# Two feed-forward networks after window attention: every network operation placed by a list scheduler at build time, one accumulator seeded by ScalarE, six weight pieces under attention

## The chip, the cores and the metric

The kernel runs on one core of one Trainium2 chip. The metric is the device time of one execution in microseconds (us); shorter is better. TensorE (PE in the profile; PEld is its weight load), VectorE (DVE), ScalarE (ACT), GpSimd (POOL) and the DMA queue of SyncE (SP) each work through their own instructions strictly in the order in which the program issued them. Semaphores tie the engines together: an instruction whose input isn't there stops everything behind it on its engine.

## The reference

Attention (4 batches, 8 heads, 512 local and 32 global tokens of dimension 64), then two feed-forward networks on its 2176 x 512 result.

```python
def _attn_ref(q_l, k_l, v_l, q_g, k_g, v_g):
    # window 32, scale 1/8; sm is a softmax over the last axis
    out_g = np.matmul(sm(scale * np.matmul(q_g, k_all.transpose(0, 1, 3, 2))), v_all)
    s_ll = np.where(mask, scale * np.matmul(q_l, k_l.transpose(0, 1, 3, 2)), -1000000000.0)
    s_l = np.concatenate([scale * np.matmul(q_l, k_g.transpose(0, 1, 3, 2)), s_ll], axis=-1)
    out_l = np.matmul(sm(s_l), np.concatenate([v_g, v_l], axis=2))
    return np.concatenate([out_g, out_l], axis=2).astype(np.float32)

def _moe_ref(x, w_in, w_out):        # network 1: 512 -> 2048 -> 512
    h = x @ w_in
    return (h * np.cos(h) @ w_out).astype(np.float32)

def _moe2_ref(x, w_in, w_out):       # network 2: the same sizes
    h = np.maximum(x @ w_in, 0.0)
    return (h * h @ w_out).astype(np.float32)
```

The weights arrive as 64-bit floats. Each 64-bit number is put together to a 32-bit one on the chip.

## The kernel before

**Attention.** A loop of 40 items (`s` in the code; 32 local halves and 8 global ones) issues, per turn and in the order of `CFG["order"]`, the stages of several items that are a few turns apart. In between it issues background work from three tables, `bga`, `bgb` and `bgc`: twelve of the 64 *pieces* of weights, the splitting of the first weights, and the preparation of the first block of x.

**A piece** (`conv_load`, `conv_a`, `conv_b`, `conv_c`) is 128 x 512 weights: a DMA of 512 KB into one of two `raw` tiles; POOL scales the high words into `cu` (line 123) and ACT the low words into `cc` (126); DVE shifts `cu` (132) and joins the sign to `cc` (133); POOL adds both into `wf` (142). Four pieces make a pair of chunks `q` (two of `w_in`, two of `w_out`), and there are 16 pairs, eight for each network.

**Splitting.** Every product runs in three passes over a high and a low part of its operands. `prep_in` makes four sums of weight blocks (`ws`, line 171), then high parts on ACT (184) and low parts by subtraction in the helper `split` (150) on DVE or POOL; `prep_out` does the same for `w_out` (`wo`). For x, `x_sum`, `x_hi`, `x_lo` do it (`xr`, `xs`), and the seven split tiles are stored to DRAM (`x_store`) and loaded again (`x_load`) for every later round over the same block. Each of the seven tiles has one buffer.

**Steps.** 48 steps follow: 8 rounds `K` (four for each network) x 3 blocks of x (2 x 384, 2 x 384 and 2 x 320 tokens) x 2 pairs `q`. A step has seven products of six matmuls (line 765), a scheme with fewer products and more additions, into four PSUM banks a, e, b, d. Between them stand additions on DVE (`add`, 779) and copies on ACT (`copy`, 773): after product 2 DVE adds `1` into b, ACT copies b to `2`, and product 4 may go on in b only after that. Each of the four results passes through `unit` (network 1: 795, 798, 803, 809; network 2: 806, 809), then a high part on ACT (818) and a low part on POOL. Then come eight (network 2: six or five) *jobs* of six matmuls (line 858), and DVE adds their results into `xt` (870).

**Order.** `lay` and `run_job` walk once over PE's work with assumed durations and give every operation of a step a time; x preparation, pieces and splitting get times by fixed offsets (`conv_a` 7.0 us after its load, `prep_in` at 2.4 us apart). All are sorted by time and issued so. Two jobs (`BACK = 2`) are held back to fill the next step's gaps. Which engine makes a sum or a low part is fixed.

Of the kernel before, what the change touches and what calls it, by code (L numbers as in the profile page):

```python
# [18 lines left out]
P = 128  # L19
# [31 lines left out]
def kernel(  # L51
# [28 lines left out]
    convp = ctx.enter_context(tc.tile_pool(name="convp", bufs=2))  # L80
# [15 lines left out]

    NQ = 2 * NC // 2
    raw, tmp, wf = {}, {}, {}  # L100
# [3 lines left out]
    def conv_load(q, m, c):  # L104
        g = 2 * q + c
        win, wout = nets[g // NC]
        f0 = (g % NC) * P
        t = convp.tile([P, DM, 2], I32, tag="raw", name="raw", bufs=2)
        flat = t.rearrange("p f w -> p (f w)")
        if m == 0:  # L110
            nc.sync.dma_start(
                flat.rearrange("p (k x) -> p k x", k=NK),
                win[:, 2 * f0 : 2 * f0 + 2 * P].rearrange("(k p) x -> p k x", p=P),
            )
        else:
            nc.sync.dma_start(flat, wout[f0 : f0 + P, :])
        raw[q, m, c] = t

    def conv_a(q, m, c):
        t = raw[q, m, c]  # L120
        u = convp.tile([P, DM], F32, tag="cu", name="cu", bufs=2)
        v = convp.tile([P, DM], U32, tag="cc", name="cc", bufs=2)
        nc.gpsimd.tensor_scalar(  # L123
            u, t[:, :, 1].bitcast(F32), 2.0**-112, 1.0, op0=ALU.mult, op1=ALU.mult
        )
        nc.scalar.activation(v, t[:, :, 0].bitcast(U32), AF.Copy, scale=2.0**-29)  # L126
        tmp[q, m, c] = (u.bitcast(U32), v)

    def conv_b(q, m, c):
        t = raw.pop((q, m, c))  # L130
        u, v = tmp[q, m, c]
        nc.vector.tensor_scalar(u, u, 3, None, op0=ALU.logical_shift_left)  # L132
        nc.vector.scalar_tensor_tensor(  # L133
            v, t[:, :, 1].bitcast(U32), 0x80000000, v,
            op0=ALU.bitwise_and, op1=ALU.bitwise_or,
        )

    def conv_c(q, m, c):
        u, v = tmp.pop((q, m, c))
        if c == 0:  # L140
            wf[q, m] = ringp.tile([P, 2, DM], F32, tag=f"wf{m}", name=f"wf{m}")
        nc.gpsimd.tensor_tensor(wf[q, m][:, c, :].bitcast(U32), u, v, op=ALU.add)  # L142
# [4 lines left out]
    SLOT = {"A11": 0, "A12": 1, "A22": 2, "S1": 3, "S2": 4, "S3": 5, "S4": 6}  # L147
# [4 lines left out]
    def prep_in(q):  # L152
        st = {}

        def sums():
            pool = pools["wa" if q % 3 < 2 else "wb"]
            WI[q] = pool.tile([P, 2, 7 * HALF], F32R, tag=f"wi{q % 3}", name="wi")
            st["s"] = ringp.tile([P, 4, HALF], F32, tag="ws", name="ws")
            f = wf[q, 0].rearrange("p c (h x) -> p c h x", h=2)
            st["f"] = f  # L160

        def s(i):
            f, t = st["f"], st["s"]
            a, b, op = (
                (f[:, 1, 0], f[:, 1, 1], ALU.add),
                (t[:, 0], f[:, 0, 0], ALU.subtract),
                (f[:, 0, 0], f[:, 1, 0], ALU.subtract),
                (f[:, 0, 1], t[:, 1], ALU.subtract),
            )[i]
            eng = nc.vector if i % 2 == 0 else nc.gpsimd  # L170
            eng.tensor_tensor(t[:, i], a, b, op=op)

        def part(k):
            f = wf[q, 0]
            return (
                (slice(0, 2 * HALF), f[:, 0, :]),
                (slice(2 * HALF, 3 * HALF), f[:, 1, HALF:]),
                (slice(3 * HALF, 5 * HALF), st["s"][:, 0:2].rearrange("p i x -> p (i x)")),
                (slice(5 * HALF, 7 * HALF), st["s"][:, 2:4].rearrange("p i x -> p (i x)")),
            )[k]  # L180

        def hi(k):
            w, x = part(k)
            nc.scalar.activation(WI[q][:, 0, w], x, AF.Copy)

        def lo(k):
            w, x = part(k)
            split(nc.gpsimd if k % 2 else nc.vector, WI[q][:, 1, w], x, WI[q][:, 0, w])

        def first():  # L190
            sums()
            s(0)
            s(2)

        def second():
            s(1)
            s(3)
            hi(0)

        def third():  # L200
            lo(0)
            hi(1)
            hi(2)

        def fourth():
            lo(1)
            lo(2)
            hi(3)

        return [first, second, third, fourth, lambda: lo(3)]  # L210

    def prep_out(q):
        def hi(c):
            if c == 0:
                pool = pools["wa" if q % 3 < 2 else "wb"]
                WO[q] = pool.tile([P, 2, 2, DM], F32R, tag=f"wo{q % 3}", name="wo")
            nc.scalar.activation(WO[q][:, 0, c, :], wf[q, 1][:, c, :], AF.Copy)

        def lo(c):
            split(  # L220
                nc.gpsimd if c else nc.vector,
                WO[q][:, 1, c, :], wf[q, 1][:, c, :], WO[q][:, 0, c, :],
            )

        return [lambda: hi(0), lambda: (lo(0), hi(1)), lambda: lo(1)]

# [442 lines left out]
    def it(k):  # L669
# [5 lines left out]
    BLOCKS = ((0, 384), (768, 384), (1536, 320))  # L675
    NG = NQ // 2
    steps = [
        (K, b, 2 * K + i) for K in range(NG) for b in range(len(BLOCKS)) for i in range(2)
    ]
    NS = len(steps)  # L680
    PROD = (
        ("B11", "A11"), ("T1", "S1"), ("T2", "S2"), ("B21", "A12"),
        ("T3", "S3"), ("B22", "S4"), ("T4", "A22"),
    )
    XPOOL = {"B11": "xa", "B21": "xa", "B22": "xa", "T1": "xb", "T2": "xc", "T3": "xc", "T4": "xc"}
    XB, XR, XS = {}, {}, {}
# [4 lines left out]
    def xraw(u, name):  # L691
        c0, n = BLOCKS[u % 3]
# [3 lines left out]
    def x_sum(u, name, kk):  # L696
        n = BLOCKS[u % 3][1]
        if kk == 0:
            XR[u, name] = pools["xb"].tile([P, 2, 384], F32, tag="xr", name="xr", bufs=3)
        src = lambda m: (XR[u, m] if m[0] == "T" else xraw(u, m))[:, kk, 0:n]  # L700
        a, b = {"T1": ("B12", "B11"), "T2": ("B22", "T1"), "T3": ("B22", "B12"), "T4": ("B21", "T2")}[name]
        eng = nc.vector if kk == 0 else nc.gpsimd
        eng.tensor_tensor(XR[u, name][:, kk, 0:n], src(a), src(b), op=ALU.subtract)

    def x_src(u, name):
        n = BLOCKS[u % 3][1]
# [6 lines left out]
    def x_hi(u, name):  # L713
        n = BLOCKS[u % 3][1]
        nc.scalar.activation(x_tile(u, name)[:, 0, :, 0:n], x_src(u, name), AF.Copy)

    def x_lo(u, name, kk):
        n = BLOCKS[u % 3][1]
        t = XB[u, name]
        split(  # L720
            nc.vector if kk == 0 else nc.gpsimd,
            t[:, 1, kk, 0:n], x_src(u, name)[:, kk], t[:, 0, kk, 0:n],
        )

    def x_store(u, name):
        n = BLOCKS[u % 3][1]
        key = net_of(u // 3), u % 3, name
# [3 lines left out]
    def x_load(u, name):  # L731
        n = BLOCKS[u % 3][1]
        t = x_tile(u, name)
        nc.sync.dma_start(
            t[:, :, :, 0:n].bitcast(F32), XS[net_of(u // 3), u % 3, name]
        )


    ops = []

    def at(t, fn):
        ops.append((t, len(ops), fn))

    GT, YB = {}, {}
    YE = 0

    class Step:
        def __init__(self, s):
# [5 lines left out]
            self.bk, self.sb, self.r = {}, {}, {}  # L754

        def prod(self, i, bank_name, start):
            x, a = PROD[i]
            n = self.n
            if start:
                self.bk[bank_name] = ps.tile([P, 512], F32, tag=LB[bank_name], name="h" + bank_name)  # L760
            out, w, xs = self.bk[bank_name][:, 0:n], WI[self.q], XB[self.u, x]
            for k in range(6):
                kk, (ws, xh) = k // 3, ((0, 0), (1, 0), (0, 1))[k % 3]
                c = SLOT[a] * HALF + kk * P
# [5 lines left out]
        def copy(self, bank_name, name):  # L770
            t = pools["s"].tile([P, 384], F32, tag=f"s{name}", name="s" + name)
            self.sb[name] = t[:, 0 : self.n]
            nc.scalar.activation(self.sb[name], self.bk[bank_name][:, 0 : self.n], AF.Copy)  # L773

        def add(self, bank_name, name, to=None):
            src = self.bk[bank_name][:, 0 : self.n]
            if to:
                self.bk[to] = ps.tile([P, 512], F32, tag=LB[to], name="h" + to)
            nc.vector.tensor_tensor(  # L779
                self.bk[to or bank_name][:, 0 : self.n], src, self.sb[name], op=ALU.add  # L780
            )

        def unit(self, t0, bank_name, f, t):

            n, V, A, G = self.n, DV(self.n), DA(self.n), DG(self.n)
            h = lambda: self.bk[bank_name][:, 0:n]
            key = bank_name

            def new_r():
                self.r[key] = pools["s"].tile([P, 384], F32, tag="cr", name="cr", bufs=4)[:, 0:n]  # L790
                return self.r[key]

            def ck():
# [386 lines left out]
```

## Time and profile before

| | us |
|---|---|
| median of 3 runs (933.03 to 938.74) | 935.76 |
| the profiled execution | 935.3 |
| its span, first to last instruction | 933.4 |
| PE busy | 870.1 (93%) |
| DVE busy | 695.8 (75%) |
| POOL busy | 561.3 (60%) |
| ACT busy | 517.4 (55%) |

The span falls into attention (to about 165 us), network 1 (four rounds, to 546 us) and network 2 (to 928 us). Matmuls overlap one another, so PE busy overstates how near PE is to its peak; the time from one matmul's start to the next is what counts. Mean TensorE clock over the span is 0.983 of the higher level (2.4 GHz).

### The profile page before, as it was taken

Reading aid. Unit: us, or ns where it says so; the run is one execution under the profiler, and the core shown is the slowest. Engines: PE = TensorE matmul, PEld = TensorE weight load, DVE = VectorE, ACT = ScalarE, POOL = GpSimd, SP = SyncE. Lnnn points to the kernel's source line nnn. Section 1 sums busy time; section 2 is a strip of 40 time slices with the busy share of each in tenths; the row PEclk is TensorE's granted clock in tenths of the full one; section 3 lists DMA queues with packets and bytes.
Section 4 is the critical chain, followed back from the end, with each engine's and each line's share of the span. In section 5 each row is a group of like instructions: output and inputs, shape, how many; then the busy total and the mean of one; then the engine's idle time right before and its main releaser. Section 6 shows DMA issues by size and latency. Waiting matters only on the chain.

```text
span 933.4 us, 17201 instructions
## 1 busy us (share of the span) xinstructions
PE 870.1 (93%) x6008; PEld 789.0 (85%) x6008; DVE 695.8 (75%) x1495; ACT 517.4 (55%) x1237; POOL 561.3 (60%) x663
## 2 busy tenths in 40 slices
PE   7798987889899999999999799999999999999997
PEld 4577765789899999999999798879888888888885
DVE  6588998489878787878797899876666666675454
ACT  4677876576675656565656465555443534353331
POOL 5498998388646554555455779875554555453231
PEclk9999999899999999999999989999999999999999
DMA  7987933365467655675567166377637863666552
GB/s 167 202 187 186 200 95 107 155 244 179 159 225 282 209 190 188 266 243 186 184 240 261 62 248 232 100 238 262 231 120 239 282 239 117 215 237 221 171 178 57
DMA packets 134311, 182.01 MB, mean 195 GB/s; under 512 B 61008, under 2 KB 114768, under 8 KB 134224
## 3 DMA queue, kind: packets, MB, share of 16 engines
q1 hardware_dynamic: 132048, 180.38, 59.4%
q8 instruction: 48, 0.79, 0.3%
q10 hardware_dynamic: 2176, 0.52, 0.3%
q14 instruction: 39, 0.32, 0.1%
HBM read 141.03 MB, written 35.65 MB: 189 GB/s over the span
## 4 chain that ended last, share of the span: by engine, by line
PE 61%; DVE 18%; POOL 8%; ACT 4%; issue 4%; DMA 2%; SPq 2%; ACTq 0%; DVEq 0%; POOLq 0%
PE y L858 30%; PE hb L765 11%; PE he L765 8%; PE ha L765 7%; POOL g L150 4%; DVE cc L133 2%; DVE pt L422 2%; POOL xs L150 1%; DVE cu L132 1%; PE s L406 1%; DVE cr L809 1%; POOL wf L142 1%; DVE xs L150 1%; ACT g L818 1%; PE o L490 1%
## 5 line engine op out<-in xcount | busy, mean ns | idle before, releaser
L150 POOL TENSOR_TENSOR g<-cr,g 128x384 fp32r<-128x384 f32 (+1 forms) x192 | 193.3, 1008 | 273.9 <-ACT g L818 250.5
L858 PE MATMUL y<-wo,g 128*128 128x512 f32 x816 | 215.7, 398 | 7.1 <-ACT g L818 4.4
L870 DVE TENSOR_TENSOR xt<-y,xt 128x384 f32<-128x384 f32 (+2 forms) x287 | 168.7, 593 | 69.1 <-PE y L858 68.6
L858 PE MATMUL y<-g,wo 128*128 128x384 f32 (+1 forms) x1152 | 218.3, 327 | 0.9 <-POOL g L150 0.9
L858 PEld LDWEIGHTS y<-g,wo 128*128 128x128 f32 x1152 | 194.6, 189 | 1.2 <-POOL g L150 1.2
L765 PE MATMUL hb<-xs,wi 128*128 128x384 f32 (+1 forms) x864 | 169.6, 331 | 15.8 <-ACT s L773 12.1
L858 PEld LDWEIGHTS y<-wo,g 128*128 128x128 f32 x816 | 150.0, 189 | 37.6 <-POOL g L150 7.7
L765 PEld LDWEIGHTS hb<-xs,wi 128*128 128x128 f32 x864 | 147.6, 190 | 26.4 <-ACT s L773 15.6
L818 ACT ACTIVATE g<-cr 128x384 fp32r<-128x384 f32 (+1 forms) x192 | 96.9, 507 | 84.2 <-DVE cr L809 82.9
L765 PE MATMUL he<-xs,wi 128*128 128x384 f32 (+1 forms) x576 | 112.9, 331 | 4.6 <-DVE cr L809 4.5
L765 PE MATMUL ha<-xs,wi 128*128 128x384 f32 (+1 forms) x576 | 111.6, 329 | 0.0
L765 PEld LDWEIGHTS he<-xs,wi 128*128 128x128 f32 x576 | 99.7, 191 | 9.8 <-DVE cr L809 5.9
L765 PEld LDWEIGHTS ha<-xs,wi 128*128 128x128 f32 x576 | 98.5, 189 | 2.3
L142 POOL TENSOR_TENSOR wf<-cu,cc 128x512 uint32<-128x512 uint32 x64 | 85.0, 1329 | 22.6 <-DVE cc L133 22.6
L803 ACT ACTIVATE cr<-cr,halfpi 128x384 f32<-128x384 f32 (+1 forms) x96 | 57.5, 599 | 38.1 <-DVE cr L798 37.5
L773 ACT ACTIVATE s<-hb 128x384 f32<-128x384 f32 (+1 forms) x48 | 22.7, 474 | 95.2 <-DVE hb L779 95.2
L123 POOL TENSOR_SCALAR cu<-raw 128x512 f32<-128x512 f32 x64 | 44.0, 688 | 26.6 <-DMA raw<-in_moe_w_in_dram 17.3
L133 DVE SCALAR_TENSOR_TENSOR cc<-raw,cc 128x512 uint32<-128x512 uint32 x64 | 58.6, 915 | 0.0
L432 ACT ACTIVATE pt<-pt,st 128x160 f32<-128x160 f32 x128 | 53.1, 420 | 6.6 <-DVE st L422 6.3
L132 DVE TENSOR_SCALAR cu<-cu 128x512 uint32<-128x512 uint32 x64 | 46.4, 724 | 6.8 <-POOL cu L123 6.6
L126 ACT ACTIVATE cc<-raw 128x512 uint32<-128x512 uint32 x64 | 42.6, 665 | 7.7 <-DMA raw<-in_moe_w_in_dram 6.1
L422 DVE CUSTOM_DVE_ANT_0 pt<-s,mask 128x160 f32<-128x160 f32 x128 | 33.7, 318 | 16.8 <-PE s L406 16.7
(125 smaller groups left out, 1337.7 us busy)
## 6 DMA issues: line engine op xcount, KB each, us to landing
xs<-xs_T SPq DMA_DIRECT2D x48, 768.0 KB, 5.8
xs<-xs_B SPq DMA_DIRECT2D x36, 768.0 KB, 5.3
raw<-in_moe_w_in_dram SPq DMA_DIRECT2D x32, 512.0 KB, 6.8
raw<-in_moe_w_out_dram SPq DMA_DIRECT2D x32, 512.0 KB, 5.2
xs<-xs_T SPq DMA_DIRECT2D x24, 640.0 KB, 6.5
xs_T<-xs SPq DMA_DIRECT2D x16, 768.0 KB, 4.1
xs<-xs_B SPq DMA_DIRECT2D x18, 640.0 KB, 5.8
xs_B<-xs SPq DMA_DIRECT2D x12, 768.0 KB, 4.0
```

The lines of the kernel that those rows point to most:

```text
L123: nc.gpsimd.tensor_scalar(u, t[:, :, 1].bitcast(F32), 2.0**-112, 1.0, op0=ALU.mult, op1=ALU.mult)
L132: nc.vector.tensor_scalar(u, u, 3, None, op0=ALU.logical_shift_left)
L133: nc.vector.scalar_tensor_tensor(v, t[:, :, 1].bitcast(U32), 0x80000000, v, op0=ALU.bitwise_and, op1=ALU.bitwise_or,)
L142: nc.gpsimd.tensor_tensor(wf[q, m][:, c, :].bitcast(U32), u, v, op=ALU.add)
L150: eng.tensor_tensor(lo, x, hi.bitcast(F32), op=ALU.subtract)
L422: nc.vector.tensor_tensor_reduce(out=self.pt[:, u, :], in0=self.s[u // 2][:, 160 * (u % 2) : 160 * (u % 2) + 160], in1=m, scale=-0.125, sc ...
L432: nc.scalar.activation(self.pt[:, u, :], self.pt[:, u, :], AF.Exp, bias=self.st[:, 0, u : u + 1], scale=-1.0, accum_out=self.st[:, 1, u : ...
L765: nc.tensor.matmul(out, lhsT=w[:, ws, c : c + P], rhs=xs[:, xh, kk, 0:n], start=start and k == 0, stop=k == 5, skip_group_check=True,)
L803: nc.scalar.activation(self.r[key], self.r[key], AF.Sin, bias=halfpi, scale=TWOPI)
L818: nc.scalar.activation(GT[k][0][:, t * n : t * n + n], self.r[key], AF.Copy)
L858: nc.tensor.matmul(o, lhsT=l, rhs=r, start=k == 0, stop=k == 5)
L870: nc.vector.tensor_tensor(dst, y, dst, op=ALU.add)
```

## The change

All operations of the networks, on every engine and on the DMA queue, become `Op` objects with needs, durations and a latest time (counted back from a walk over PE's work). A list scheduler places them in simulated time: an engine that is free takes, of the operations that are ready, the one with the earliest latest time. Sums and low parts may go to DVE or POOL (`opVG`), whichever the plan picks. All are issued in the order of their planned starts. On PE the products keep their order, and jobs stay three behind the rate at which they come in (`KEEP`).

From step 2 on, bank b starts from a copy of bank a that ACT writes straight into it (`seed`), and product 2 accumulates on that; the DVE addition after it and the copy `1` are gone. b and d swap banks from step to step. The weight tile of a pair is cut into four tiles. `conv_a` and `conv_b` become four operations; `cu` is gone, since POOL scales straight into the tile of `wf`. `w_out`'s two pieces have a tile each.

Attention carries six pieces in place of twelve: pair 0 whole and `w_in` of pair 1, loaded every third item. The other six, and the splitting of pair 1's `w_out`, go into the plan. Of the sums of these two pairs one each moves from DVE to POOL. The stores of the first x block are issued at the end of attention, ahead of the plan.

```diff
-    t = convp.tile([P, DM, 2], I32, tag="raw", name="raw", bufs=2)
+    ATT = [(0, 0, 0), (0, 0, 1), (0, 1, 0), (0, 1, 1), (1, 0, 0), (1, 0, 1)]
...
-    def conv_a(q, m, c):
-        u = convp.tile([P, DM], F32, tag="cu", name="cu", bufs=2)
+    def conv_u(q, m, c):
+        u = conv_to(q, m, c)
+        G.tensor_scalar(u, t[:, :, 1].bitcast(F32), 2.0**-112, 1.0, op0=ALU.mult, op1=ALU.mult)
...
+    SEM = 0.2
+    d_mm = lambda n: n * 0.000414 + 0.0147
+    d_act = lambda n: 0.17 + n * 0.00084
+    d_ps = lambda n: 0.14 + n * 0.0011
+    d_v2 = lambda n: 0.2 + n * 0.0018
+    d_g2 = lambda n: 0.1 + n * 0.0024
...
+    def opVG(n, fn, *needs):
+        return Op({"G": d_g2(n), "V": d_v2(n)}, lambda e: fn(V if e == "V" else G), *needs)
+    def opQ(kb, fn, *needs):
+        return Op({"Q": kb / 330.0}, lambda e: fn(), *needs, lag=2.0)
...
+        def seed(self):
+            A.activation(self.hold("b"), self.hold("a"), AF.Copy)
...
+                if i == 0:
+                    if s < SEEDED:
+                        o["s1"] = opA(da, lambda: self.copy("a", "1"), p, free_s.get("1"))
+                    else:
+                        o["s1"] = opA(da, self.seed, p, bank_free.get(B_))
+                elif i == 2:
+                    b = p
+                    if s < SEEDED:
+                        p.after(bank_free.get(B_))
+                        b = free_s["1"] = opV(d1, lambda: self.add("b", "1", "b"), p, o["s1"])
+                    else:
+                        p.after(o["s1"])
+                    o["s2"] = opA(da, lambda: self.copy("b", "2"), b, free_s.get("2"))
+                    o["e"] = opV(d1, lambda: self.add("e", "2", "e"), o["s2"], o["s5"])
+                elif i == 4:
+                    p.after(o["s2"])
+                    o["d"] = opV(d1, lambda: self.add("b", "5", "d"), p, o["s5"], bank_free.get(D_))
...
+    def conv(q, m, c):
+        ld = opQ(525.0, lambda: conv_load(q, m, c), *free)
+        u = opG(0.75, lambda: conv_u(q, m, c), ld, *wfree)
+        s = opA(0.67, lambda: conv_s(q, m, c), ld, *cfree)
+        v = opV(0.76, lambda: conv_v(q, m, c), u)
+        o = opV(1.0, lambda: conv_o(q, m, c), s, u)
+        end = opG(1.33, lambda: conv_c(q, m, c), v, o)
...
+    KEEP = 3
+    def target(s, i):
+        lo, hi = (njobs[s - 1] if s else 0), njobs[s]
+        return lo + (hi - lo) * i / 7.0 - KEEP
...
+        f = free_at[e]
+        t = max(f, min(o.at for o in ready[e]))
+        can = [o for o in ready[e] if o.at <= t]
+        o = min(can, key=lambda o: (o.latest, o.key))
...
+    placed.sort(key=lambda o: (o.start, o.key))
...
-    for i in range(12):
-        q, (m, c) = i // 4, PIECES[i % 4]
-        s = 5 + 2 * i + (i // 4)
+    for i, k in enumerate(ATT):
+        s = 5 + 3 * i
+        put(bga, s, lambda k=k: conv_load(*k))
+        put(bga, s + 2, lambda k=k: conv_u(*k))
+        put(bga, s + 2, lambda k=k: conv_s(*k))
+        put(bgb, s + 3, lambda k=k: conv_v(*k))
+        put(bgb, s + 3, lambda k=k: conv_o(*k))
+        put(bgc, s + 4, lambda k=k: conv_c(*k))
...
+            for m, _, _ in PROD:
+                x_store(0, m)
```

## Rows read from the trace of the kernel before

**Rows 1.** Chain of waits: start us, duration us, what; jobs of 512, 384, 320 columns.

```profile
631.06 1.39 PE y L858 x6
...
291.62 2.08 PE y L858 x12
...
276.60 1.75 PE y L858 x12
```

**Rows 2.** Windows, one round K each: length, busy us (instructions), granted clock, DMA share, GB/s.

```profile
165.30:263.80 98.50, 90.40 (x575) 85.84 (x576) 75.28 (x135) 63.18 (x130) 66.61 (x63) 0.97 0.53 192
263.80:355.20 91.40, 89.69 (x542) 89.11 (x542) 73.95 (x138) 54.53 (x112) 49.67 (x51) 1.00 0.63 223
...
446.60:546.20 99.60, 92.48 (x542) 91.24 (x542) 82.75 (x150) 58.26 (x117) 62.05 (x61) 0.97 0.53 193
546.20:646.20 100.00, 95.21 (x487) 85.06 (x487) 82.11 (x126) 54.96 (x111) 79.33 (x74) 0.97 0.59 203
646.20:738.30 92.10, 90.44 (x458) 79.41 (x457) 62.12 (x102) 40.88 (x87) 49.15 (x51) 1.00 0.63 214
...
830.70:928.40 97.70, 96.20 (x488) 85.09 (x486) 49.30 (x83) 34.00 (x72) 26.33 (x28) 1.00 0.50 160
```

**Rows 3.** Timeline of PE: start, us, instruction [idle time before it, what ended it].

```profile
165.21 0.48 PE L475 MATMUL tg<-ident,pg 128*128 128x128 f32 x1 [4.21 <-ACT tgs L484]
...
348.91 1.14 PE L765 MATMUL hb<-xs,wi 128*128 128x320 f32 x6 [1.68 <-ACT s L773]
...
537.70 1.97 PE L765 MATMUL hb<-xs,wi 128*128 128x320 f32 x6 [5.56 <-ACT s L773]
...
576.79 2.29 PE L765 MATMUL hb<-xs,wi 128*128 128x384 f32 x6 [2.19 <-DVE hd L779]
...
617.70 2.50 PE L858 MATMUL y<-wo,g 128*128 128x512 f32 x4 [2.00 <-ACT g L818]
```

**Rows 4.** Chain of waits from 519 to 541 us, the end of round 3.

```profile
532.35 1.48 DVE cc L133
...
535.70 1.07 DVE xs L150
536.77 0.42 DVE hb L779
```

**Rows 5.** Windows in attention, columns as in rows 2.

```profile
24.60:56.80 32.20, 26.00 (x401) 21.25 (x400) 19.43 (x99) 21.06 (x80) 18.35 (x38) 0.95 0.99 208
56.80:141.20 84.40, 73.75 (x1123) 58.08 (x1122) 79.73 (x288) 67.36 (x240) 79.16 (x134) 0.98 0.68 158
```

**Rows 6.** Groups by form, whole span: count, busy us, mean ns, idle before it.

```profile
L123 POOL TENSOR_SCALAR cu<-raw 128x512 f32<-128x512 f32 x64 | 44.0, 688 | 26.6 <-DMA raw<-in_moe_w_in_dram 17.3 <-DMA raw<-in_moe_w_out_dram 8.1 <-PE ha L765 1.2
...
L142 POOL TENSOR_TENSOR wf<-cu,cc 128x512 uint32<-128x512 uint32 x64 | 85.0, 1329 | 22.6 <-DVE cc L133 22.6
...
L132 DVE TENSOR_SCALAR cu<-cu 128x512 uint32<-128x512 uint32 x64 | 46.4, 724 | 6.8 <-POOL cu L123 6.6
...
L133 DVE SCALAR_TENSOR_TENSOR cc<-raw,cc 128x512 uint32<-128x512 uint32 x64 | 58.6, 915 | 0.0
...
L150 POOL TENSOR_TENSOR wo<-wf,wo 128x512 fp32r<-128x512 f32 x16 | 21.2, 1326 | 0.0
...
L150 DVE TENSOR_TENSOR wo<-wf,wo 128x512 fp32r<-128x512 f32 x16 | 11.9, 743 | 0.0
...
L779 DVE TENSOR_TENSOR hb<-hb,s 128x384 f32<-128x384 f32 x32 | 17.9, 560 | 9.2 <-PE hb L765 8.8 <-issue 0.4
...
L773 ACT ACTIVATE s<-ha 128x384 f32<-128x384 f32 x32 | 15.3, 479 | 5.1 <-PE ha L765 5.1
```

**Rows 7.** Tile raw, 0 to 200 us: DVE's join there, min/median/max ns.

```profile
L133 DVE SCALAR_TENSOR_TENSOR cc<-raw,cc x12: 672/679/876, 39.0 to 134.7; 128x512 uint32<-128x512 uint32 x12
```

**Rows 8.** Tile raw, 265 to 530 us: its DMAs.

```profile
DMA to landing us min/median/max: 3.6/7.6/9.7
```

**Rows 9.** Chain of waits from 20 to 60 us.

```profile
39.96 5.29 DMA raw<-in_moe_w_in_dram
```

More of the change, by code (lines that the diff above doesn't have):

```diff
@@ L149, in split @@
+    SLOT = {a: (i, j) for i, part in enumerate(PARTS) for j, a in enumerate(part)}
     def split(eng, lo, x, hi):
         eng.tensor_tensor(lo, x, hi.bitcast(F32), op=ALU.subtract)
[L152 to L210, printed above, removed]
@@ new lines, in w_in @@
+    def w_in(q):
+        ends = [conv(q, 0, c) for c in range(2)]
+        sums = {}
+        for i, needs in ((0, []), (2, [0]), (1, [0]), (3, [1])):
+            o = opVG(256, lambda eng, i=i: w_sum(q, i, eng), *ends, *[sums[k] for k in needs])
+            if i == 0:
+                o.after(*w_free["ws"])
+            sums[i] = o
+        last = max((s for s in range(NS) if steps[s][2] == q - 3), default=None)
+        used = []
+        for k, i in ((0, 3), (1, 2), (2, 5), (3, 6)):
+            n = HALF * len(PARTS[k])
+            src = ends if k in (0, 3) else [sums[2 * k - 2], sums[2 * k - 1]]
+            h = opA(d_act(n), lambda k=k: w_hi(q, k), *src, prods.get((last, i)))
+            lo = opVG(n, lambda eng, k=k: w_lo(q, k, eng), h)
+            wi_ready[q, k] = lo
+            used.append(lo)
+        w_free["wf0"], w_free["ws"] = used + list(sums.values()), used + list(sums.values())
@@ new lines, in w_out @@
+    def w_out(q):
+        ends = [conv(q, 1, c) for c in range(2)]
+        last = max((s for s in range(NS) if steps[s][2] == q - 3), default=None)
+        lo = []
+        for c in range(2):
+            h = opA(d_act(512), lambda c=c: o_hi(q, c), ends[c], *g_free.get(last, []))
+            if c:
+                h.after(lo[0].needs[0])
+            o = opVG(512, lambda eng, c=c: o_lo(q, c, eng), h)
+            wf1_ring.free[WJ[q, c]] = [o]
+            lo.append(o)
+        wo_ready[q] = Op({"N": 0.0}, lambda e: None, *lo)
@@ new lines @@
+    RJ.update({k: (i % 2, i % 2) for i, k in enumerate(ATT)})
+    WJ.update({(0, 0): 0, (0, 1): 1})
+    XRJ.update({(0, m): j for m, j in (("T1", 0), ("T2", 1), ("T3", 2), ("T4", 0))})
+    xr_ring.i = 1
+    w_out(1)
+    for s in range(NS):
+        K, b, q = steps[s]
+        if s % 2 == 0 and s:
+            x_prep(s // 2)
+        S[s].plan()
+        if K < NG - 1:
+            if s % 6 == 0:
+                w_in(2 * K + 2)
+                w_out(2 * K + 2)
+            elif s % 6 == 5:
+                w_in(2 * K + 3)
+        if K and s % 6 == 0:
+            w_out(2 * K + 1)
@@ new lines @@
+    KEEP = 3
+    njobs = [sum(w.s < s for w in jobs) for s in range(NS + 1)]
+    def target(s, i):
+        lo, hi = (njobs[s - 1] if s else 0), njobs[s]
+        return lo + (hi - lo) * i / 7.0 - KEEP
+    order = [(s, i) for s in range(NS) for i in range(7)]
+    t, j = 0.0, 0
+    for s, i in order:
+        while j < target(s, i):
+            jobs[j].latest = t
+            t += jobs[j].on["P"]
+            j += 1
+        prods[s, i].latest = t
+        t += prods[s, i].on["P"]
+    for w in jobs[j:]:
+        w.latest = t
+        t += w.on["P"]
@@ new lines @@
+    BIAS = 6.0
+    count = len(allops)
+    while count:
+        picks = [(b[0], e, b[1]) for e in ready for b in [best(e)] if b]
+        t, e, o = min(picks, key=lambda x: (x[0], x[2] is None))
+        if o is None:
+            free_at[e] = max(t, free_at[e])
+            continue
+        for x in o.on:
+            if o in ready[x]:
+                ready[x].remove(o)
+        o.start, o.end, o.eng = t, t + o.on[e], e
+        if e != "N":
+            free_at[e] = o.end
+        placed.append(o)
+        count -= 1
+        if e == "P":
+            if nxt < len(order) and o is prods[order[nxt]]:
+                nxt += 1
+            else:
+                jdone += 1
+        for y in o.users:
+            missing[y.key] -= 1
+            if missing[y.key] == 0:
+                release(y)
@@ L1053 @@
     put(bgb, 37, lambda: x_hi(0, "T1"))
-    for kk in range(2):
-        put(bgb, 38, lambda kk=kk: x_lo(0, "T1", kk))
+    for kk, eng in enumerate((V, G)):
+        put(bgb, 38, lambda kk=kk, eng=eng: x_lo(0, "T1", kk, eng))
     L = CFG["lag"]
```

612 lines of the change are left out of this document (360 added, 252 removed).

## The prediction

> **What bounds the kernel now.** I read the windows by round first, then PE's timeline for the gaps, then the chain of waits behind the largest gap, then attention's windows, and last the groups by form for prices.
>
> From one matmul's start to the next a run of six takes 1.39 us at 512 columns, and two runs take 2.08 us at 384 and 1.75 at 320 [rows 1]: 0.232, 0.173 and 0.146 us a matmul. A step of network 1 has 42 + 48 matmuls of one width, 15.6 us at 384 and 13.1 at 320; a step of network 2 has 42 of its width and 36 (30) of 512, 15.6 and 13.1 again. A round has four wide steps and two narrow ones: 88.6 us that nothing in the change touches, 709 us for eight rounds. The rounds fill 165.3 to 928.4 us, 763 us. So 54 us of the networks are gaps or slow matmuls, and that is what an order of instructions can win back.
>
> Where they are [rows 2]: the second round (the third is alike) lasts 91.4 us, 2.8 over the 88.6; the fourth 99.6 (11.0 over), the fifth 100.0 (11.4), the sixth (the seventh is alike) 92.1 (3.5). The first lasts 98.5, but pushes the ten jobs of 320 columns at its end into its successor (60 x 0.146 = 8.8 us), so it is 18.7 over 79.8; the last, 97.7, holds such a rest and is nearly full.
>
> The gaps look alike [rows 3]. Product 4 into b waits 1.68 us (second round) and 5.56 us (fourth) for ACT's copy of b. The chain at the 5.56 us shows who was late: not ACT, but DVE, whose addition into b (0.42 us) stood in its queue behind the join of a piece (1.48 us) and a low part of x (1.07 us) [rows 4], none of them urgent. PE isn't short of work in total, DVE isn't full (74 of 91 us in a round [rows 2]); the order in DVE's queue is wrong for a few us at a time.
>
> In attention it is different: from 56.8 to 141.2 us DVE is busy 79.7 and POOL 79.2 of 84.4 us, PE 73.8 [rows 5]. There the two engines are the bound. Before 56.8 us the DMA queue is: its share is 0.99 [rows 5], and a late load of a piece holds the chain for 5.29 us [rows 9].
>
> **The change, part by part.** The sum is made against the profiled execution's 935.3 us (0.5 below the median; 1.9 us lie outside its span).
>
> *Six pieces leave attention.* A piece costs POOL 0.69 + 1.33 = 2.02 us and DVE 0.72 + 0.92 = 1.64 us [rows 6]. Ten of the twelve lay in the stretch from 56.8 us; four will. Pair 1's `w_out` takes a low part of 1.33 us off POOL and one of 0.74 off DVE [rows 6]; two sums of half that width go from DVE to POOL, by half those prices 0.4 and 0.7 us each. POOL: 79.2 - 12.1 - 1.3 + 1.3, about 67. DVE: 79.7 - 9.8 - 0.7 - 0.7, about 68. Then PE with 73.8 is the longest. The tightest engine now is busy 94% of the stretch; at that share PE's work takes 78 us, 6 less than 84.4. In the early stretch two loads fewer and a use that lies one turn later take 1 us off the 5.29. I take -7, with -11 (PE at 100%) and -2 (the early stretch and SP's queue set the pace) as ends.
>
> *The first round takes them up.* DVE and POOL are busy 75.3 + 66.6 = 141.9 us there [rows 2]. Added: 6 x (2.02 + 1.64) = 22 and 2 us for `w_out` of pair 1; off: four additions of 0.56 [rows 6]. That gives 164 us for two engines, nearly what the fifth round carries now (82.1 + 79.3 = 161.4, in 100.0 us). At the fifth round's fill (0.81) 164 us last 101; at 94%, which attention shows to be possible, 87. What isn't due can slip into the second round, where the two are busy 124 of 183 us. I take 0 for the round, ends -5 and +6: a better order of more work. The stores of the first block now stand ahead of the plan's loads on SP, so the first two pieces' loads start some us after the plan's zero; ACT and POOL mostly wait for attention's tail then (PE stands for 4.21 us just before [rows 3], which the change leaves alone).
>
> *The seed.* ACT's copy `1` costs 0.48 us [rows 6] and becomes a copy into PSUM. No row shows ACT writing PSUM. DVE's addition with a PSUM result takes 0.56 us [rows 6], 0.08 more than ACT's copy; so 0.40 to 0.56, and I take 0.48, as the row of the same engine and source. 46 of these by 0.08 are 4 us on ACT, which is busy 54 of 91 us a round, so nothing on the path. What goes is 46 DVE additions, 25 us of DVE, and the place of these additions in the chain product 2, addition, copy, product 4: the two gaps above had just this addition late. What is new is that product 2 waits for ACT's seed; product 1 and one or two jobs (2 to 3 us) stand between, against 0.5 us of copy. Behind the waiting product 2 all of PE queues.
>
> *The order.* Second and third round: the gap of 1.68 goes, the small ones stay: -1.5 each, -3 together (ends -5 and +1). Fourth and fifth: 22.4 us over. The x tiles have one buffer each, so all seven must be made anew between a product of one step and the same product of the next, about 13 us; ACT's seven high parts and 14 low parts fit only just beside the step's own work. I leave 8 us of the 22.4: -14. The ends are -19 (as good as the second round) and -5 (only the 5.56 goes). Sixth and seventh: -2 each, since three jobs held back cover the waits for g (2.00 us in the fifth round [rows 3]) better than two: -4 (ends -6 and 0). Last: -0.5 (ends -1.5 and 0).
>
> Sum: -7 + 0 - 3 - 14 - 4 - 0.5 = -28.5. 935.3 - 28.5 = 906.8, about 907 us.
>
> **The rivals.**
>
> *The loads land later than planned: slower.* The plan has a load of a piece land 525 / 330 + 2.0 = 3.6 us after it starts, and puts POOL's and ACT's part right there. Loads land after 3.6, 7.6 (median), 9.7 us [rows 8]; the old order left 7.0. If the plan's queue doesn't see the crowd that makes the difference, ACT and POOL stand still with the seed or a copy behind the piece. PE has some 2.4 us of cover (a product and two jobs, less a copy). 58 pieces at a lateness of 3.1 us lose 0.7 each, 41 us: 935.3 - 28.5 + 41 = 948. It decides from 28.5 / 58 = 0.5 us a piece, a lateness of 2.9. For it speaks the distance from 3.6 to 7.6; against it, that 3.6 is just what an undisturbed load takes and that the plan, too, makes loads wait for one another. 8%.
>
> *DVE and POOL hinder each other.* DVE's join takes 0.67 us in attention [rows 7] and 0.92 over the span [rows 6], 1.48 in the crowded fourth round [rows 4]. So a plan that runs DVE and POOL side by side, with one fixed price each, is too tight where both are full. Then the first round grows by 6 and the fourth and fifth give 7 less: 907 + 13 = 920. The Trainium skill speaks for this rival: SBUF — State Buffer, "Who interferes with whom", has a DVE instruction with two SBUF inputs and a GpSimd instruction that reads SBUF contend for one port pair, and the second stands until the first is through. By that rule low parts on DVE would win nothing in a full round, and the time would be this rival's 920 and not 907. The trace agrees in part: 0.67 turns into 1.48, yet the fifth round gets 161 us of both done in 100. 15%.
>
> *The order does nothing:* the waits are for data, not for places in queues. Then attention gives 7, the first round takes 6: 934. Against it stands the chain in rows 4. 7%.
>
> *Everything fits:* all the lower ends, -11 - 5 - 5 - 19 - 6 - 1.5 = -47.5: 888. 10%.
>
> **How the numbers follow.** The forecast has 60%. Its own spread is 892 to 921. The range of 889 to 934 takes in the second and third rival, most of the bounds, and leaves out some of the slower and of the fastest case. About 0.5% (4.7 us) is what a measurement of this kernel can tell from no change. Faster by more: 60 + 15 + 10 = 85%; within: 7%; slower: 8%.
>
> **What would show it.** Right: the gaps before product 4 into b are gone, and no large ones stand before product 2; the second round lasts near 90 us, fourth and fifth together near 186; the loop from 56.8 us in attention is 6 us shorter; DVE has 46 additions less. Wrong: POOL's or ACT's piece work waits for DMA in most rounds (first rival); low parts on DVE near 1.2 us and gaps for `he` and g in the first and fifth round (second); gaps of the old sizes at new places (third).

## The result, and the profile after

The changed kernel takes 894.4 us (median of 4 runs, 892.45 to 894.74) against 935.6: a ratio of 0.9554, 95% interval 0.9521 to 0.9586. The forecast was 907 with a range of 889 to 934; it gained 41 us where 28.5 were forecast. The profiled execution took 894.67 us with a span of 892.7.

Windows by round, columns as in rows 2 (length; busy time of PE, PEld, DVE, ACT and POOL; granted clock; DMA share; GB/s): the first two, the third, the fifth and the sixth round after.

```profile
154.30:241.00 86.70, 83.56 (x539) 80.12 (x540) 69.80 (x118) 61.87 (x127) 75.88 (x73) 0.98 0.67 242
241.00:335.90 94.90, 92.44 (x554) 90.94 (x554) 77.66 (x139) 58.82 (x126) 72.19 (x70) 1.00 0.62 220
335.90:421.40 85.50, 85.50 (x518) 85.50 (x517) 66.91 (x125) 52.07 (x110) 60.07 (x58) 1.00 0.66 234
...
512.80:610.70 97.90, 94.97 (x512) 87.38 (x511) 82.93 (x125) 55.44 (x115) 93.05 (x85) 0.98 0.61 216
610.70:699.40 88.70, 88.70 (x457) 79.75 (x457) 56.14 (x92) 42.44 (x88) 53.51 (x54) 1.00 0.64 215
```

The networks begin at 154.3 us instead of 165.3, and the sixth round lasts 88.7 us, the floor, where it lasted 92.1 [rows 2]. The other rounds can't be compared by length alone, because the plan pushes a varying number of jobs into the next round (518 to 554 matmuls in these windows, 540 belong to a round of network 1). So I take a measure that doesn't depend on that: for each matmul of the networks the time from its start to the next one's start, less the 0.232, 0.173 or 0.146 us of its width [rows 1], summed by round. These are the gaps in the table; with 709 us of matmuls and the networks' start they give the end. All later figures of gaps in this text go by it.

| us | networks start | round 1 | 2 | 3 | 4 | 5 | 6 | 7 | 8 | gaps |
|---|---|---|---|---|---|---|---|---|---|---|
| before | 165.3 | 18.5 | 2.8 | 2.8 | 11.0 | 9.6 | 3.5 | 3.8 | 2.0 | 53.9 |
| after | 154.3 | 12.1 | 4.5 | 0.7 | 1.8 | 5.4 | 0.1 | 0.0 | -0.2 | 24.4 |

So 11.1 us come from attention and 29.5 from the networks, 40.6 of the 40.7 us by which the span shrank.

A gap in this sense is not only idle time. In both kernels some 5 us of round 1's figure are the last 93 matmuls of attention, which run between the products of the first step. And where the granted clock is 0.50 (the lower level, 1.2 GHz), matmuls are slow without a pause: from the starts of the matmuls in these stretches I estimate 7.5 us of this kind in the networks before and 3.3 us after. So about 4 of the 29.5 us are time at the lower clock that is gone.

The largest gaps of rounds 2 and 5 after, from PE's timeline (as in [rows 3]). In this kernel's lines L807 is a product, L818 the seed, L815 a copy, L821 an addition, L850 the last reading of a bank, L858 a high part of g, L899 a job, L910 its addition into `xt`:

```profile
278.91 1.32 PE L899 MATMUL y<-g,wo 128*128 128x384 f32 x6 [0.96 <-DVE xt L910]
283.99 1.31 PE L807 MATMUL hb<-xs,wi 128*128 128x384 f32 x6 [1.31 <-ACT hb L818]
...
554.41 1.28 PE L807 MATMUL hb<-xs,wi 128*128 128x384 f32 x6 [1.00 <-DVE hd L821]
560.39 2.13 PE L807 MATMUL ha<-xs,wi 128*128 128x384 f32 x6 [1.94 <-DVE cr L850]
```

The 5.56 us of round 4 and the 1.68 us of round 2 have no successor at product 4 (the one wait there, 1.01 us, is in the first step, which isn't seeded); the new wait, product 2 on the seed (L818), shows with 1.31 us and once more with 0.21.

Attention after, windows of the same items as rows 5:

```profile
24.80:53.60 28.80, 25.97 (x399) 21.09 (x398) 19.55 (x96) 20.53 (x79) 16.74 (x35) 0.94 0.87 195
53.60:130.40 76.80, 72.33 (x1124) 57.80 (x1123) 67.03 (x281) 63.19 (x233) 65.89 (x128) 0.98 0.66 147
```

The long stretch went from 84.4 to 76.8 us, the early one from 32.2 to 28.8. DVE fell from 79.7 to 67.0, POOL from 79.2 to 65.9, and PE is now the engine that fills 94% of the stretch.

### The profile page after: what moved, and what is told of

Read it like the earlier page. It is cut to its first block, busy times and chain, and to the rows that moved or that the text cites. A ratio compares the mean times of both kernels' runs of the same rounds, so it can differ in the third digit from the quotient of the medians.

```text
span 892.7 us, 17179 instructions
## 1 busy us (share of the span) xinstructions
PE 858.0 (96%) x6008; PEld 786.7 (88%) x6008; DVE 649.5 (73%) x1403; ACT 512.7 (57%) x1241; POOL 612.9 (69%) x705
## 5 line engine op out<-in xcount | busy, mean ns | idle before, releaser
L168 POOL TENSOR_TENSOR g<-cr,g 128x384 fp32r<-128x384 f32 (+1 forms) x192 | 201.7, 1063 | 130.6 <-ACT g L858 128.0
L910 DVE TENSOR_TENSOR xt<-y,xt 128x384 f32<-128x384 f32 (+2 forms) x287 | 170.5, 595 | 95.6 <-PE y L899 94.6
L899 PE MATMUL y<-g,wo 128*128 128x384 f32 (+1 forms) x1152 | 219.6, 327 | 2.4 <-DVE xt L910 1.0
L899 PE MATMUL y<-wo,g 128*128 128x512 f32 x816 | 210.0, 394 | 0.0
L899 PEld LDWEIGHTS y<-g,wo 128*128 128x128 f32 x1152 | 194.1, 188 | 3.3 <-DVE xt L910 1.3
L899 PEld LDWEIGHTS y<-wo,g 128*128 128x128 f32 x816 | 150.7, 189 | 24.4
L807 PE MATMUL hb<-xs,wi 128*128 128x384 f32 (+1 forms) x864 | 166.6, 327 | 3.6 <-ACT hb L818 1.5
L807 PEld LDWEIGHTS hb<-xs,wi 128*128 128x128 f32 x864 | 146.8, 188 | 10.4 <-ACT hb L818 2.2
L807 PE MATMUL ha<-xs,wi 128*128 128x384 f32 (+1 forms) x576 | 112.9, 331 | 1.9 <-DVE cr L850 1.9
L807 PE MATMUL he<-xs,wi 128*128 128x384 f32 (+1 forms) x576 | 111.8, 329 | 1.4 <-DVE cr L850 1.3
L858 ACT ACTIVATE g<-cr 128x384 fp32r<-128x384 f32 (+1 forms) x192 | 93.2, 500 | 20.4 <-DVE cr L850 17.3
L159 POOL TENSOR_TENSOR wf<-wf,cc 128x512 uint32<-128x512 uint32 x64 | 88.3, 1383 | 23.9 <-DVE wf L147 23.9
L807 PEld LDWEIGHTS he<-xs,wi 128*128 128x128 f32 x576 | 98.8, 189 | 6.6 <-DVE cr L850 2.8
L807 PEld LDWEIGHTS ha<-xs,wi 128*128 128x128 f32 x576 | 99.0, 190 | 5.0 <-DVE cr L850 2.9
L844 ACT ACTIVATE cr<-cr,halfpi 128x384 f32<-128x384 f32 (+1 forms) x96 | 56.1, 592 | 12.2 <-DVE cr L839 11.4
L138 POOL TENSOR_SCALAR wf<-raw 128x512 f32<-128x512 f32 x64 | 47.7, 755 | 17.8 <-DMA raw<-in_moe_w_out_dram 10.0
L815 ACT ACTIVATE s<-hb 128x384 f32<-128x384 f32 (+1 forms) x48 | 22.6, 472 | 51.2 <-PE hb L807 51.1
L147 DVE TENSOR_SCALAR wf<-wf 128x512 uint32<-128x512 uint32 x64 | 45.5, 714 | 1.4 <-POOL wf L138 1.4
L168 POOL TENSOR_TENSOR wi<-ws,wi 128x512 fp32r<-128x512 f32 x24 | 31.8, 1329 | 20.1 <-ACT wi L192 16.2
```

What stands on the lines that cost most here:

```text
L138: G.tensor_scalar(u, t[:, :, 1].bitcast(F32), 2.0**-112, 1.0, op0=ALU.mult, op1=ALU.mult)
L147: V.tensor_scalar(u, u, 3, None, op0=ALU.logical_shift_left)
L159: G.tensor_tensor(u, u, v, op=ALU.add)
L168: eng.tensor_tensor(lo, x, hi.bitcast(F32), op=ALU.subtract)
L807: nc.tensor.matmul(out, lhsT=w[:, ws, c : c + P], rhs=xs[:, xh, kk, 0:n], start=start and k == 0, stop=k == 5, skip_group_check=True,)
L844: A.activation(self.r[key], self.r[key], AF.Sin, bias=halfpi, scale=TWOPI)
```

## The experiments

Theory: the gaps came from the order in DVE's, ACT's and POOL's queues, and the plan's priorities repair it; the seed and the six pieces pay only because the plan can use the room. Rivals: the seed itself removes the gaps at product 4; attention's 11 us are a gain whatever the networks do; the free choice between DVE and POOL is what counts; the held jobs are. Each run below gives its time, and the ratio of it to the kernel before with the 95% interval.

**The seed alone.** The kernel before, with the seed in its old plan:

```diff
             if i == 0:
-                at(e, lambda: st.copy("a", "1"))
-                hold[3] = e + A
+                if s < 2:
+                    at(e, lambda: st.copy("a", "1"))
+                    hold[3] = e + A
+                else:
+                    t = max(e, bank_free.get(bn["b"], 0.0))
+                    at(t, st.seed)
+                    hold[2] = hold[3] = t + A
...
+                w = V if s < 2 else 0.0
+                if s < 2:
+                    at(e, lambda: st.add("b", "1"))
```

> The kernel before with one part of the change: from step 2 on ScalarE seeds b, and b and d swap banks; times in its plan moved accordingly, nothing else. If DVE's addition in the chain to product 4 made the gaps there (13.4 us in eight gaps of before), they vanish and the time is near 922. If the order of DVE's queue is the cause whatever stands in it, the late additions into d and e take their place and the time stays within 930 to 936.

936.5 us, ratio 1.0004 (0.9982 to 1.0025): nothing. PE's timeline at the end of round 4 (the stretch of rows 4, which counts rounds from 0), and the chain of waits behind it (L779 is the seed here, L787 the addition into d):

```profile
527.74 1.14 PE L767 MATMUL hb<-xs,wi 128*128 128x320 f32 x6 [2.11 <-ACT hb L779]
540.66 1.97 PE L767 MATMUL hb<-xs,wi 128*128 128x320 f32 x6 [5.63 <-DVE hd L787]
```

```profile
535.19 0.95 DVE xs L150
536.14 1.13 DVE wi L150
537.27 1.27 DVE xr L703
...
539.34 0.47 DVE xs L150
...
540.20 0.42 DVE hd L787
```

The addition into b is gone, and the next addition, from b into d, is late in its place: 5.63 us at product 6 instead of 5.56 at product 4, and 2.11 us more where product 2 waits for the seed. The queue holds the same low parts and sums ahead of the urgent addition. Rounds 2 and 3 gained 1.5 us each; rounds 1 and 8 lost 1.9 and 1.6.

**The plan without the seed.** The kernel after with `SEEDED = NS`.

> The kernel after with the addition into b and the copy 1 in all steps (no seed). If the scheduler's order does the work, it finds a place for the additions too: 894 to 898. If the seed carries a good part, the gaps before product 4 come back: 904 or more.

901.4 us, ratio 0.9636 (0.9601 to 0.9670): 7 us slower than the kernel after, between the two expectations. The gaps rise from 24.4 to 31.7 us, in round 2 (7.8 against 4.5), 3 (2.2 against 0.7) and 5 (7.8 against 5.4). PE waits for the copy behind the addition again, but briefly; round 3:

```profile
380.34 1.31 PE L807 MATMUL hb<-xs,wi 128*128 128x384 f32 x6 [1.15 <-ACT s L815]
```

So the seed is worth nothing in the old order and 7 us in the new one: once the queues are in order, one step less on DVE in the chain to product 4 counts.

**Six pieces alone.** The kernel before, attention with six pieces, the others in round 1 by the old offsets:

```diff
-    for i in range(12):
+    for i in range(6):
...
+        if K == 0:
+            for c in range(2):
+                conv(0.5 + 3.0 * c, 1, 1, c)
+            spread(16.0, 2.4, prep_out(1))
+        for i, (m, c) in enumerate(PIECES):
+            conv(t0 + (0.2 if K else 0.7) * w + 0.5 * w * i, qa, m, c)
```

> The kernel before with six pieces in attention (spaced as in the kernel after), the other six and the splitting of pair 1's w_out put into the first round by the old fixed offsets. If attention gains 11 and the first round takes the work for nothing, 925. If the old order can't place it, attention ends near 154 us and the first round grows by 8 or more: 932 or above.

934.9 us, ratio 0.9990 (0.9967 to 1.0013): nothing. The networks start at 153.0, 12.3 us earlier, and round 1's gaps rise from 18.5 to 29.7 us, round 2's from 2.8 to 4.3. The round's window and PE's timeline in it:

```profile
153.00:262.70 109.70, 95.36 (x575) 91.26 (x576) 85.90 (x145) 65.89 (x134) 75.79 (x72) 0.91 0.52 188
```

```profile
185.75 2.29 PE L765 MATMUL hb<-xs,wi 128*128 128x384 f32 x6 [2.79 <-DVE hd L779]
195.20 1.88 PE L765 MATMUL he<-xs,wi 128*128 128x384 f32 x6 [2.53 <-DVE cr L809]
214.11 1.31 PE L765 MATMUL he<-xs,wi 128*128 128x384 f32 x6 [1.45 <-DVE cr L809]
224.79 1.65 PE L765 MATMUL hb<-xs,wi 128*128 128x384 f32 x4 [4.16 <-ACT s L773]
```

DVE and POOL carry 161.7 us in 109.7, a fill of 0.74 (of the two engines' time), and PE stands for 2.8, 2.5, 1.5 and 4.2 us behind work in their queues. After three of these pauses the matmuls are slow (six take 2.29 and 1.88 us, four take 1.65), where the six after 1.45 us take 1.31: the granted clock of the round is 0.91.

**The plan with twelve pieces in attention.** The kernel after, with `ATT` of twelve pieces, pair 1's `w_out` split in attention again, and the plan without them.

> The kernel after with all twelve pieces and pair 1's w_out in attention again, the plan without them. If DVE and POOL bound attention, it ends near 165 us again; the first two rounds, 16.6 us over their floor in the kernel after, give at most 4 back: 901 to 905. If the moved work was what the first two rounds' gaps came from, they give more than 8 back: 897 or less.

904.0 us, ratio 0.9661 (0.9627 to 0.9696). The networks start at 163.4; the gaps are 24.7 us, as good as the same: round 1 gives 0.7 us back and round 2 2.6, rounds 3 and 5 lose 1.1 and 2.5. So under the plan the six pieces cost the networks next to nothing, and the 9 us they free in attention stay. But the plan doesn't keep every queue in order. In round 5 of this run a pause of the old size stands at product 6; PE's timeline there, and the chain of waits before it:

```profile
570.02 2.29 PE L807 MATMUL hb<-xs,wi 128*128 128x384 f32 x6 [5.56 <-DVE hd L821]
```

```profile
564.41 2.81 DVE xs L168 x2
567.21 1.68 DVE wo L168
...
569.49 0.48 DVE hd L821
```

The two low parts of x took 2.81 us on DVE, for which the plan had counted 1.78 (`d_v2(384)` twice), and the low part of `wo` 1.68, counted as 1.12 and 0.74 on average before [rows 6]. So the urgent addition stood behind work that took longer than planned; whether that is all of the 5.56 us, no run shows.

The four runs together: pieces and seed each bring 0 in the old order, 9.6 and 7 in the plan. What is left of the 41, some 24 us, is the plan's by difference, together with the finer weight tiles that came with it; no run had the plan without both parts, or the old order with those tiles.

**Fixed engines.** The kernel after, each sum and low part on the engine it had before:

```diff
-    def opVG(n, fn, *needs):
-        return Op({"G": d_g2(n), "V": d_v2(n)}, lambda e: fn(V if e == "V" else G), *needs)
+    def opVG(n, fn, *needs, on):
+        d = {"G": d_g2(n), "V": d_v2(n)}[on]
+        return Op({on: d}, lambda e: fn(V if e == "V" else G), *needs)
```

> The kernel after, but each sum and low part has the engine that the kernel before gave it (the plan may choose only the time). If the time of each operation is what the plan brings, 894 to 898. If the choice of the engine is needed where DVE and POOL are both full, the first, second and fifth round (12.1, 4.5 and 5.4 us of gaps in the kernel after) get gaps of 8 us more together: 903 or more.

894.2 us, ratio 0.9547 (0.9524 to 0.9569), gaps 23.1: the free choice brings nothing.

**First come, first served.** The kernel after; a free engine takes what became ready first (the edit stands in two places). One rule by the latest time is left: DVE leaves to POOL what isn't due within 6 us.

```diff
-        o = min(can, key=lambda o: (o.latest, o.key))
+        o = min(can, key=lambda o: (o.at, o.key))
```

> The kernel after, but a free engine takes the operation that became ready first, not the one with the earliest latest time. If urgency is what repairs the queues, gaps of 1 to 3 us come back in most rounds, at the products that wait for e, d and the copies: 910 or more. If following readiness is enough, 894 to 900.

913.8 us, ratio 0.9760 (0.9742 to 0.9779): 19 us slower than the kernel after, 22 faster than before. The gaps are 43.5 us: 26.7 in round 1 (12.1), 11.8 in round 5 (5.4), and no more than without the edit in the others. PE's timeline in round 1, and the chain of waits before its last line:

```profile
171.11 1.33 PE L807 MATMUL hb<-xs,wi 128*128 128x384 f32 x6 [2.14 <-DVE hd L821]
177.07 2.19 PE L807 MATMUL he<-xs,wi 128*128 128x384 f32 x6 [3.59 <-DVE cr L850]
...
199.85 1.32 PE L807 MATMUL he<-xs,wi 128*128 128x384 f32 x6 [2.63 <-DVE cr L850]
203.22 2.29 PE L807 MATMUL hb<-xs,wi 128*128 128x384 f32 x6 [2.05 <-ACT hb L818]
```

```profile
197.63 1.28 POOL xs L168
198.91 1.15 POOL xr L681
200.06 0.97 POOL g L168
201.03 0.69 POOL ws L181
201.75 0.63 ACT wi L192
202.38 0.41 ACT g L858
202.79 0.39 ACT hb L818
```

The seed, which product 2 waits for, stands on ACT behind a high part of weights of a later pair, which stands behind a sum on POOL. In rounds 1 and 5, with much side work, urgency is worth the 19 us; in the other rounds readiness is enough.

**One job held back.** `KEEP = 1` in place of 3.

> The kernel after with one job held back in place of three. If the held jobs cover the waits for g, the sixth and seventh round, which have no gaps in the kernel after, get back 3 us each, and the others as much: 910 or more. If priorities alone cover g, at most 4 more: 898.

891.4 us, ratio 0.9523 (0.9506 to 0.9541): not slower, if anything 3 us faster (the intervals of the two ratios overlap). The networks start 1.2 us earlier here and the gaps are 1.9 us less. Rounds 6 and 7 stay without gaps (0.1 and 0.0), so three held jobs aren't needed to close them. They are closed in the first-come kernel too, which holds three, so the priorities aren't needed either; whether one of the two must be there, no run shows. What is left of the plan (jobs spread evenly over the products, a job taken wherever a product isn't ready) wasn't taken apart.

**Loads that land later in the plan.** `lag=5.0` in place of 2.0 for DMAs.

> The kernel after with 5.0 us in place of 2.0 from a load's transfer to its use in the plan. ACT and POOL wait 23 us in all for the loads of pieces in the kernel after. If these waits are off PE's path, the time stays within 892 to 897 though they shrink. If they cost, 890 or less; if later use starves the splitting, 898 or more.

895.6 us, ratio 0.9570 (0.9549 to 0.9592): no difference. The waits for loads of pieces, first in the kernel after, then in this run (engine and line, waited for: us in total, times, longest):

```profile
ACT cc L143 <- DMA raw<-in_moe_w_out_dram: 10.8, 6, 4.2
POOL wf L138 <- DMA raw<-in_moe_w_out_dram: 10.0, 7, 4.4
ACT cc L143 <- DMA raw<-in_moe_w_in_dram: 5.0, 6, 1.9
POOL wf L138 <- DMA raw<-in_moe_w_in_dram: 3.3, 4, 1.2
```

```profile
POOL wf L138 <- DMA raw<-in_moe_w_out_dram: 5.4, 3, 4.2
ACT cc L143 <- DMA raw<-in_moe_w_out_dram: 1.4, 1, 1.4
POOL wf L138 <- DMA raw<-in_moe_w_in_dram: 1.1, 1, 1.1
ACT cc L143 <- DMA raw<-in_moe_w_in_dram: 0.2, 1, 0.2
```

29 us of waiting over the whole span (23.0 of them in the networks, the figure of the expectation) became 8, and the time stayed. It isn't that nothing else moved: the networks start 2.2 us earlier and round 5's gaps grow from 5.4 to 7.7 us, with pauses of 1.77 and 1.79 us for the splitting of `w_out`. So some of the expected harm from later use is there, in one round. That leaves single waits that may count, which the next run looks at.

**Attention's end.** In the kernel after ACT stands 3.95 us for the high part of T4 ahead of copies that PE waits for, and 4.18 us for the first piece, whose load stands behind the stores on SP. ACT's and PE's timelines after:

```profile
152.57 0.84 ACT L693 ACTIVATE xs<-xr 128x768 fp32r<-128x768 f32 x1 [3.95 <-POOL xr L681]
164.88 0.67 ACT L143 ACTIVATE cc<-raw 128x512 uint32<-128x512 uint32 x1 [4.18 <-DMA raw<-in_moe_w_out_dram]
```

```profile
154.12 0.47 PE L453 MATMUL tg<-ident,pg 128*128 128x128 f32 x1 [4.36 <-ACT tgs L462]
```

Both moved:

```diff
+        if s == NI:
             x_hi(0, "T4")
             for kk, eng in enumerate((V, G)):
                 x_lo(0, "T4", kk, eng)
+        if s == NI + 1:
             for m, _, _ in PROD:
                 x_store(0, m)
```

> The kernel after with two places of attention's end changed: the high part of T4 (the operand of product 6) is issued one item later, so ScalarE no longer stands 3.95 us ahead of the copies that PE's 4.36 us of idle time wait for; and the stores of the first x block are issued behind the plan's first loads, so the piece whose conversion held ScalarE 4.18 us lands earlier. If both stand on the path, 5 to 7 us: 887 to 890. If the first round is bound by DVE and POOL anyway, the gain is lost again there: 893 or more.

891.0 us, ratio 0.9535 (0.9511 to 0.9559): 3 us where 5 to 7 were expected. The networks start at 147.1, 7 us earlier (in runs that leave attention alone the start lies between 152.1 and 155.2), but round 1's gaps grow from 12.1 to 15.0 and its first step from 15.2 to 18.2 us. ACT's and PE's timelines:

```profile
162.00 0.67 ACT L143 ACTIVATE cc<-raw 128x512 uint32<-128x512 uint32 x1 [4.92 <-DMA raw<-in_moe_w_out_dram]
```

```profile
165.24 2.29 PE L807 MATMUL ha<-xs,wi 128*128 128x384 f32 x6 [3.91 <-DVE cr L850]
```

Only one of the two loads got ahead of the stores; ACT stands for the second, and PE for ACT 3.91 us. The two products after this pause run at the lower clock, 2.29 us for six matmuls.

**The same with one job held.**

> As the run before, with one job held back too (3 us by itself). If the two gains add, 884 to 888. If both win back the same gaps of the first two rounds, as the run before.

889.1 us, ratio 0.9514 (0.9488 to 0.9540), with the same 4 us gap after the first step (3.88). The full sum of the two gains would be 888.0, which the interval doesn't exclude; so they add, nearly or wholly.

**Both loads ahead of the stores.** As the run before, one held job included; the stores one turn later (`NI + 2`).

> As the run before, but the stores stand one more turn later, behind both loads of the plan's first two pieces. In the run before only one of the two was ahead of the stores, the other landed late, and ScalarE stood at the second conversion (4.9 us), PE 3.9 us for it before the next step. If that wait is on the path: 885 to 887. If the next wait (sine's table load, the conversions on DVE) takes its place, 888 to 890.

886.0 us (884.52 to 886.87), ratio 0.9482 (0.9451 to 0.9514). The gap of 3.88 us is gone, the networks start at 149.7 (147.5 in the run before), and the gaps are 20.5 us, 11.4 of them in round 1. Windows of its first two rounds:

```profile
149.70:237.50 87.80, 83.57 (x552) 80.32 (x551) 79.51 (x126) 64.86 (x134) 82.69 (x77) 1.00 0.65 237
237.50:324.70 87.20, 86.81 (x524) 86.55 (x523) 69.32 (x127) 56.58 (x121) 67.57 (x66) 1.00 0.69 244
```

DVE and POOL carry 162.2 us in 87.8 us, a fill of 0.92, at the clock's higher level throughout. This version is faster than both kernels.

## Why the prediction was right, and where it was off

**Attention** (-7, ends -11 and -2): -11.1. The mechanism and its sizes in the long stretch hold: POOL 65.9 for 67 forecast, DVE 67.0 for 68, PE at 94% of the stretch as assumed; 7.6 us for the 6 forecast. The term that was mis-sized is the early stretch, 3.4 us for 1: there the DMA queue's share fell from 0.99 to 0.87 and the 5.29 us hold [rows 9] is gone.

**First round** (0, ends -5 and +6): -6.4. It lies outside its ends, and this is the step that failed. I sized a full round by the fill that the old order reached in round 5 (0.81), as if the order weren't what is being changed. The run with six pieces alone shows the old order with that load: +11.2. The plan does it with less than the old gaps, and puts part of the load into round 2, whose DVE and POOL carry 149.9 us instead of 123.6 [rows 2]. The 0.94 that I kept as the other end is near what the last run reached, 0.92.

**The seed.** Its price was right: 0.476 us a copy into PSUM at 384 columns, beside the 0.479 of the copy it replaces [rows 6]; in the kernel after, groups by form:

```profile
L818 ACT ACTIVATE hb<-ha 128x384 f32<-128x384 f32 x30 | 14.3, 476 | 7.9 <-PE ha L807 7.8
```

Taking the addition off the chain wasn't given a term of its own, and its part under the plan is 7 us. That the gap would only move to the next addition in the old order I hadn't said.

**Rounds 2 and 3** (-3): -0.4. Round 3 gained 2.1 of its 2.8; round 2 lost 1.7 to the work that slipped into it, so it lasts 93 us by this measure and not near 90 as I had named for a sign. **Rounds 4 and 5** (-14, ends -19 and -5): -13.4, and 7.2 us of gaps are left where I had left 8. That this fits so well is partly luck: the 22.4 us I started from were lengths, and the fifth round's 11.4 hold 1.8 us of jobs that the fourth had pushed into it; by gaps the two rounds had 20.6. And they are distributed otherwise: round 4 is nearly clean, round 5 keeps 5.4. **Rounds 6 and 7** (-4, ends -6 and 0): -7.2. The size was too small and the reason wrong: three held jobs aren't needed, as the run with one shows; what closed them stays open. **Round 8** (-0.5): -2.2.

So the sum was 28.5 and is 40.7: +4 from attention, +6.4 from the first round, +3.2 from rounds 6 and 7, +1.7 from the last, -2.6 from rounds 2 and 3, -0.6 from 4 and 5.

**The rivals.** The late loads exist: ACT and POOL wait 29 us for them. They are off the path for the most part, apart from the first two pieces, which cost 3 us behind the stores. In the prediction this was said (the stores stand ahead of the plan's loads) and then set aside because ACT mostly waits for attention's tail; it waits for that and then for the load. The lateness of 3.1 us that gave this rival its 948 wasn't worked out from a row; the median of [rows 8] is 4.0 us over the plan.

DVE and POOL do hinder each other. POOL's low part of g takes longer after (1.125 us on average at 384 columns, 1.056 before). Of the 64 joins on DVE in the kernel after, the 11 that no instruction of POOL overlaps took 0.67 to 0.68 us, the other 53 took 0.97 on average. The longest, from DVE's and POOL's timelines:

```profile
726.95 1.80 DVE L152 SCALAR_TENSOR_TENSOR cc<-raw,cc 128x512 uint32<-128x512 uint32 x1
726.91 1.29 POOL L159 TENSOR_TENSOR wf<-wf,cc 128x512 uint32<-128x512 uint32 x1
```

POOL's addition was there first and ends at 728.20; the join ends 0.55 us later. The joins of 1.78, 1.55, 1.40, 1.33 and 1.24 us also end 0.55 us after POOL's instruction. By the Trainium skill's page SBUF — State Buffer, "Who interferes with whom", a DVE instruction with two SBUF inputs contends with a GpSimd instruction that reads SBUF, and the lock is exclusive. These joins agree with that.

So the second rival's mechanism is real, but it didn't cost what the rival said (920 us). That 162 us of busy time of both fit into 87.8 is no proof by itself, since an instruction that stands for the other counts as busy. What limits the cost are the gaps that are left: 24.4 us in the kernel after, 20.5 in the last run, some 5 of them attention's matmuls. The run with twelve pieces shows one place, in round 5, where DVE's stretched low parts stand ahead of a pause of 5.56 us. Of the signs named for this rival, low parts of x on DVE took 1.22 us at 320 columns, but only 0.88 at 384.

## What to carry to other kernels

An engine that is 80% busy on average can still be the bound, if its queue puts side work ahead of what the critical engine waits for: look in the chain of waits at what stood before the late instruction. Removing that one late instruction moves the gap to the next of its kind; order the queue by how late each operation may be, and only then shorten chains and move work, since both brought nothing here before and 7 and 10 us afterwards. When the change is the order itself, don't size a full stretch by the fill that the old order reached.

## What the runs showed of the hardware

A copy on ACT from one PSUM bank to another costs no more than one into SBUF (0.476 against 0.490 us at 384 columns, `s<-hb` in the same run). A join on DVE that meets an addition of POOL under way ends 0.55 us after it; alone it takes 0.67 us.

After a pause of PE the granted clock is sometimes 0.50, the lower of its two levels (1.2 GHz), and six matmuls of 384 columns then take up to 2.29 us instead of 1.3. Windows over two such sixes of the first-come run:

```profile
199.85:201.17 1.32, 1.32 (x6) 0.99 (x6) 1.32 (x4) 0.50 (x1) 1.32 (x3) 0.98 0.97 396
203.22:205.51 2.29, 2.29 (x7) 2.29 (x8) 1.83 (x3) 1.94 (x4) 2.29 (x3) 0.50 0.12 48
```

The first came after a pause of 2.63 us, the second after another of 2.05. So the last pause alone doesn't tell: in the same run six matmuls took 1.33 us after 2.14, and 2.29 after 1.20 that followed one of 1.96. After the pauses of 2.79, 3.59, 3.91, 4.16 and 5.56 us in these runs the matmuls were slow each time. A long pause can cost a microsecond more than its length.
